# Pairing head h with head h + 4 in the last four attention chunks, with split loads of q and k and x written back to neighbours

## The chip, the cores and the metric

The kernel runs on one core of one Trainium2 chip. The metric is the device time of one execution in microseconds (us). Its engines run side by side and meet at semaphores: PE (TensorE, matmuls), PEld (its weight loads), DVE (VectorE), ACT (ScalarE), POOL (GpSimd) and SP (SyncE, which here only issues DMAs). An engine carries out its own instructions in order.

## The reference

The input is q, k and v for 4 batches of 8 heads, 768 positions and 64 values a head. Heads 0, 2 and 6 are retrieval heads with plain causal attention. The other five are streaming heads: a query sees the last 64 positions and the first 4 (the sinks). The result goes through a two-layer MLP.

```
retr = is_retrieval                    # [1, 0, 1, 0, 0, 0, 1, 0]
keep = causal & (retr | pos_k < 4 | pos_q - pos_k < 64)
a = softmax(where(keep, q @ k.T / 8, -1e9))          # per batch and head
x = (a @ v).transpose(0, 2, 1, 3).reshape(3072, 512)
h = x @ w_in                            # 512 -> 2048
out = maximum(0.01 * h, h) @ w_out      # 2048 -> 512
```

## The kernel before

The 3072 rows are worked in 8 chunks of 384 positions, in the order batch 0, batch 1 (first halves), batch 0, batch 1 (second halves), then the same for batches 2 and 3. So chunks 4 and 5 are first halves and 6 and 7 second halves of batches 2 and 3; a second half has more keys.

One loop iteration n does the MLP of chunk n (in_slots at L548, sixteen units of four 384-column matmuls; out_slots at L573, sixteen units of 512-column matmuls, one chunk behind) and, between these units, the attention of chunk n + 1. merge (L606) lays the two lists out by hand. From iteration 3 on, the last nine MLP units come after the last attention slot. In iteration n also the loads of chunk n + 3 and the transposes of chunk n + 2 are issued.

The path of q and k of a chunk is: load_qk (L107) casts fp32 to bf16 during a DMA from POOL's queue, one transfer of 128 KB for each of three position tiles; turn_dma (L221) lets SP issue a DMA transpose of the whole chunk, which puts two heads on the 128 partitions of each of four pairs; spreads (L228) lets DVE copy each half of the keys into a zero-padded buffer kt, so that one pair's q serves either head. load_v and v_shift bring v, once as it is and once shifted by half a tile. load_qk has one buffer for k and one for q, so a chunk's load waits until the transpose before it has read the buffer.

Attention (L275) makes units for each head: retr, with full score tiles, and stream, six 64-column score matmuls. Each unit's scores go through exp on ACT and a mask on DVE, and the AV matmuls (L295) follow two slots later. The units of a pair gather in one PSUM bank po. The sink scores of all heads come from one unit, sink (L301): four matmuls, one for each pair, with ksink as weights, in which every head has four columns of its own. finish (L383) adds the sink AV of a pair (65 columns for a pair with one streaming head, 130 for one with two), takes the reciprocal of the sums and multiplies (L394) into xs. x_t (L397) transposes xs into xt, from chunk 4 on by a DMA transpose that SP issues, one for each pair as soon as it is finished. sink_keys_by (L254) fills ksink: its zeros are set once at the start, and two small copies for each batch put in the keys.

The pairs before are (0, 1), (2, 3), (4, 5), (6, 7): each has at least one streaming head. The lines that order pairs and sinks:

```
for h in order:                                              # order = range(H)
    if seen == {0, 1} or (2 in seen and h == 1):
        units.append((self.sink, None, None))
...
last = {p: max([sink_at] + [j for j, u in enumerate(units) if u[2] == p]) for p in range(4)}
```

Of the kernel before, what the change touches and what calls it, by code (L numbers as in the profile page):

```python
# [12 lines left out]
BF16 = mybir.dt.bfloat16  # L13
ACTF = mybir.ActivationFunctionType
ALU = mybir.AluOpType
# [6 lines left out]
def kernel(  # L22
# [12 lines left out]
    nc = tc.nc  # L35
# [49 lines left out]
    vs = [bf(f"vs{i}", H, D + 1) for i in range(2)]  # L85
    ksink = [bf(f"ksink{i}", 4 * SK) for i in range(2)]
    ats = [bf(f"ats{i}", 3, 4, 64) for i in range(5)]
    ats4 = [bf(f"ats4{i}", 4, 4, 64) for i in range(2)]
    w_in_bf = bf("w_in_bf", KG, DF)
    w_out_bf = bf("w_out_bf", NG, DM)  # L90

# [3 lines left out]
    k0 = rot.tile([128, 3, H, D], BF16, name="k0", tag="kd", bufs=2)  # L95
    q0 = rot.tile([128, 3, H, D], BF16, name="q0", tag="qd", bufs=3)
    f0 = {nm: rot.tile([128, DM], FP32, name="o", tag="o", bufs=6).rearrange("p (h d) -> p h d", h=H) for nm in ("k", "q")}

    def load_first(nm):
        for eng, h in ((nc.sync, slice(0, 4)), (nc.scalar, slice(4, 8))):  # L100
# [6 lines left out]
    def load_qk(n, nms="kq"):  # L107
        b, c = ORDER[n]
        for nm in nms:
            t = rot.tile([128, 3, H, D], BF16, name=f"{nm}b", tag=f"{nm}b", bufs=1)  # L110
            raw[nm, n] = t
            for g in range(3):
                nc.gpsimd.dma_start(out=t[:, g], in_=nat[nm][b, c, :, :, g])  # L113

    def load_v(n, gs=range(3)):
        b, c = ORDER[n]
# [137 lines left out]
    def sink_keys_by(b):  # L254

        ks, kk = ksink[b % 2], kt[b % 2]

        def odd():
            nc.vector.tensor_copy(ks[64:128, :].rearrange("p (q t) -> p q t", t=SK)[:, :, NS : 2 * NS],
                                  kk[64:128, :, 1, 0:NS])  # L260

        def even():
            nc.vector.tensor_copy(ks[0:64, 256 + 4 * NS : 256 + 5 * NS], kk[0:64, 2, 0, 0:NS])

        return [odd, even]

    def sink_keys(b):
        for f in sink_keys_by(b):
# [6 lines left out]
    class Attention:  # L275
        def __init__(self, n, score_tags=("psS",), po_tags=("po", "po", "po", "po"), xt_eng="a", cross=False):
            self.n = n
            self.b, self.c = ORDER[n]
            self.i = self.b % 2
            xts[n] = rot.tile([128, 4, CH], BF16, name="xt", tag="xt", bufs=2)  # L280
            self.po = {}
            self.tags = score_tags
            self.po_tags = po_tags
            self.sc = 0
            self.xt_eng = xt_eng
            self.cross = cross
            self.sink_lo = 128 if self.c == 0 else 0
            self.units = {h: (self.retr(h) if IS_RETR[h] else self.stream(h)) for h in range(H)}
# [12 lines left out]
        def sink(self):  # L301
            i, c = self.i, self.c
            s = self.score()
            w = CH - self.sink_lo
            for p in range(4):
                nc.tensor.matmul(s[:, 0:w], lhsT=ksink[i][:, 128 * p : 128 * p + 128], rhs=q_of(self.n, p, self.sink_lo, CH),  # L306
                                 start=(p == 0), stop=(p == 3))
            self.at_sink = rot.tile([128, CH], BF16, name="at_sink", tag="at_sink", bufs=2)
            nc.scalar.activation(out=self.at_sink[:, self.sink_lo : CH], in_=s[:, 0:w], func=ACTF.Exp, scale=SM)

        def retr(self, h):
            p, hh = divmod(h, 2)
            i, c, n = self.i, self.c, self.n
            groups = [[(0, 0)], [(1, 128), (2, 256)]] if c == 0 else \
                [[(kj, 0)] for kj in range(4)] + [[(4, 128), (5, 256)]]
            r = []
            for grp in groups:
                box = {}

                def qk(grp=grp, box=box):  # L320
                    s = self.score()
                    a = rot.tile([128, CH], BF16, name="at", tag="at", bufs=6)
                    off = 0
                    for j, (kj, lo) in enumerate(grp):
                        w = CH - lo
                        nc.tensor.matmul(  # L326
                            s[:, off : off + w], lhsT=kt[i][:, p, hh, 128 * kj : 128 * kj + 128],
                            rhs=q_of(n, p, lo, CH), start=(j == 0), stop=(j == len(grp) - 1),
                            skip_group_check=True)
                        off += w  # L330
                    nc.scalar.activation(out=a[:, 0:off], in_=s[:, 0:off], func=ACTF.Exp, scale=SM)  # L331
                    if len(grp) == 2:
                        d = a.rearrange("p (j t) -> p j t", j=3)[:, 0:3:2, :]
                        nc.vector.tensor_mul(d, d, m_caus.rearrange("p (o t) -> p o t", o=1).to_broadcast([128, 2, 128]))  # L334
                    elif grp[0][0] >= 3 * c:
                        nc.vector.tensor_mul(a[:, 0:128], a[:, 0:128], m_caus[:])  # L336
                    box[0] = a

                def do_av(grp=grp, box=box):
                    off = 0  # L340
                    for (kj, lo) in grp:
                        for qi in range(lo // 128, 3):
                            o = off + 128 * qi - lo
                            self.av(p, hh, qi, box[0][:, o : o + 128], va[self.b][:, kj, h, :])
                        off += CH - lo

                r.append((qk, do_av, p))
            return r

        def stream(self, h):  # L350
            p, hh = divmod(h, 2)
            i, c, n = self.i, self.c, self.n
            box = {}

            def qk():
                s = self.score()
                a = ats[ats_i[0] % len(ats)]
                ats_i[0] += 1
                for m in range(6):
                    k0 = 64 * max(6 * c + m - 1, 0)  # L360
                    nc.tensor.matmul(  # L361
                        s[:, 64 * m : 64 * m + 64], lhsT=kt[i][:, p, hh, k0 : k0 + 128],
                        rhs=q_of(n, p, 64 * m, 64 * m + 64), start=(m == 0), stop=(m == 5),
                        skip_group_check=True)
                av_ = a[:, :, 0:4:3, :]
                nc.scalar.activation(  # L366
                    out=av_, in_=s[:, 0:CH].rearrange("p (j e f) -> p j e f", j=3, e=2),
                    func=ACTF.Exp, scale=SM)
                m_ = (m_win0 if c == 0 else m_win).rearrange("p (j e) f -> p j e f", j=3)
                nc.vector.tensor_mul(av_, av_, m_)  # L370
                box[0] = a

            def do_av():
                a = box[0]
                for j in range(3):
                    t = 3 * c + j
                    ve = va[self.b][:, 0, h, :] if t == 0 else vb[self.b][:, t - 1, h, :]
                    self.av(p, hh, j, a[:, j, 0:2, :], ve)
                    self.av(p, hh, j, a[:, j, 2:4, :], va[self.b][:, t, h, :])

            return [(qk, do_av, p)]

        def finish(self, p):  # L383
            for j in range(self.sink_lo // 128, 3):
                a = self.at_sink[:, 128 * j : 128 * j + 128]
                if IS_RETR[2 * p]:
                    self.av(p, 1, j, a, vs[self.i][:, 2 * p + 1, :])
                else:
                    self.av(p, None, j, a, vs[self.i][:, 2 * p : 2 * p + 2, :])
            po = self.po[p]  # L390
            linv = rot.tile([128, 3, 2], FP32, name="linv", tag="linv", bufs=2)
            nc.vector.reciprocal(linv[:], po[:, :, :, D])  # L392
            xs = rot.tile([128, 3, 2, D], BF16, name="xs", tag="xs", bufs=4)
            nc.vector.tensor_tensor(xs[:], po[:, :, :, 0:D], linv.to_broadcast([128, 3, 2, D]), op=ALU.mult)  # L394
            return xs

        def x_t(self, p, xs, tag="psS", eng="a"):  # L397
            if self.cross:
                nc.sync.dma_start_transpose(out=xts[self.n][:, p, :].rearrange("p (j t) -> p j t", j=3),
                                            in_=xs.rearrange("p j h d -> p (j h d)"))  # L400
# [6 lines left out]
            else:  # L407
                nc.vector.tensor_copy(xts[self.n][:, p, :], pt[:, 0, 0:3, :])

        def slots(self, order=range(H), lag=2):  # L410
            units = []
            seen = set()
            for h in order:
                if seen == {0, 1} or (2 in seen and h == 1):
                    units.append((self.sink, None, None))
                seen.add(h)
                units += self.units[h]
            sink_at = [j for j, u in enumerate(units) if u[1] is None][0]
            last = {p: max([sink_at] + [j for j, u in enumerate(units) if u[2] == p]) for p in range(4)}
            LAG, X = lag, 0 if self.cross else 3  # L420
            r, box = [], {}
            for t in range(len(units) + LAG + X):
# [23 lines left out]
    class First:  # L446
        def __init__(self, j):
# [1 line left out]
            self.at_of, self.po, self.xs = {}, {}, {}  # L449
            self.qs = slice(128 * j, 128 * j + 128)  # L450
            if j == 0:
                self.at = rot.tile([128, H, 128], BF16, name="at8", tag="at8", bufs=1)
            else:
                self.blocks = [(kj, h) for kj in range(j, -1, -1) for h in RETR] + [None]
                self.at = bf(f"at_first{j}", len(self.blocks), 128)
# [364 lines left out]
```

## Time and profile before

| | us |
|---|---|
| median of 9 runs | 235.99 |
| lowest, highest | 235.22, 236.66 |
| the profiled execution's own time | 235.35 |
| its span, first to last instruction | 233.6 |
| busy in the span: PE | 224.5 |
| ACT | 127.8 |
| DVE | 97.1 |
| POOL (its DMA issues included) | 71.5 |

The granted TensorE clock was 1.00 of full speed. The busy times are sums over the whole span; what a change is worth in one stage has to be read from the timeline of that stage. A merged line of the timeline gives the start, the length and how many instructions were put together; some matmul records (a few per cent) are missing, so a group of three can show as two. A name like kt<-kd reads "kt written from kd".

### The profile page before, as it was taken

How to read it: one execution, taken by the hardware profiler on the slowest of the kernel's cores; microseconds unless marked ns; L12 is line 12 of the kernel's file. 1: busy time of each engine (PE TensorE's matmuls, PEld its weight loads, DVE VectorE, ACT ScalarE, POOL GpSimd, SP SyncE). 2: the span in 40 equal slices, each digit the busy share in tenths (PEclk: the TensorE clock that was granted, in tenths of full speed). 3: DMA queues.
4: the chain of work that ended last, by engine and by line, in shares of the span. 5: the costliest groups of instructions: out<-in, count | busy, mean ns of one | idle time of the engine just before them, and what ended most of it. 6: DMA issues, size and time to landing. Idle time of an engine off the chain costs nothing.

```text
span 233.6 us, 5091 instructions
## 1 busy us (share of the span) xinstructions
PE 224.5 (96%) x2054; PEld 140.0 (60%) x2080; DVE 97.1 (42%) x281; ACT 127.8 (55%) x276; POOL 71.5 (31%) x87
## 2 busy tenths in 40 slices
PE   8799899999999999999999999999999999999995
PEld 5689566645665676566556655656556665555554
DVE  7778676034456252666324451155213341111122
ACT  4665857714764887655355544766466763434300
POOL 8986625048149069167005800000000000000000
DMA  9999999999999999989949992920210221111112
GB/s 130 151 183 165 203 207 167 175 148 174 143 242 195 167 182 137 184 134 164 129 97 190 175 165 58 207 65 17 79 48 0 65 65 35 45 45 45 45 47 90
DMA packets 109479, 28.97 MB, mean 124 GB/s; under 512 B 101248, under 2 KB 105744, under 8 KB 109456
## 3 DMA queue, kind: packets, MB, share of 16 engines
q0 software_dynamic: 77088, 13.39, 74.6%
q1 hardware_dynamic: 31312, 15.00, 30.7%
q10 hardware_dynamic: 1056, 0.26, 0.6%
q8 instruction: 16, 0.26, 0.5%
q14 instruction: 7, 0.06, 0.1%
HBM read 27.30 MB, written 6.29 MB: 144 GB/s over the span
## 4 chain that ended last, share of the span: by engine, by line
PE 92%; ACT 3%; DVE 2%; issue 1%
PE py L580 31%; PE ph L554 30%; PE po L295 6%; PE psS L326 5%; PE psS L580 3%; PE psS L361 3%; PE ph L567 2%; PE psS L554 2%; PE psS L151 2%; PE psS L306 2%; ACT at L331 1%; PE py L213 1%; PE psS L404 1%; ACT g L556 1%; PE po L511 1%
## 5 line engine op out<-in xcount | busy, mean ns | idle before, releaser
L554 PE MATMUL ph<-xt,w_in_bf 128*128 128x384 bf16 x448 | 90.5, 326 | 0.0
L580 PE MATMUL py<-w_out_bf,g 128*128 128x512 bf16 (+1 forms) x326 | 85.7, 374 | 1.4
L556 ACT ACTIVATE g<-ph 128x384 bf16<-128x384 f32 x112 | 55.0, 492 | 56.6 <-PE ph L554 55.9
L554 PEld LDWEIGHTS <-w_in_bf 128*128 128x128 bf16 x480 | 44.1, 98 | 31.2 <-issue 0.2
L580 PEld LDWEIGHTS <-g 128*128 128x128 bf16 x416 | 35.7, 98 | 25.6
L331 ACT ACTIVATE at<-psS 128x384 bf16<-128x384 f32 x78 | 36.7, 490 | 15.7 <-PE psS L326 15.4
L586 DVE COPY o<-py 128x512 f32<-128x512 f32 (+1 forms) x22 | 14.9, 679 | 53.0 <-PE py L580 52.6
L113 POOL DMA_DIRECT2D kb<-in_k_dram x21 | 18.7, 904 | 39.0 <-DMA kd<-kb 38.0
L326 PE MATMUL psS<-qd,kt 128*128 128x384 bf16 (+2 forms) x90 | 22.8, 294 | 0.0
L118 POOL DMA_DIRECT2D va<-in_v_dram x24 | 21.5, 919 | 2.5 <-DMA w_out_bf<-in_moe_w_out_dram 1.8
L113 POOL DMA_DIRECT2D qb<-in_q_dram x21 | 18.6, 913 | 5.4 <-DMA w_in_bf<-in_moe_w_in_dram 1.8
L295 PE MATMUL po<-va,at 128*128 128x65 bf16 x228 | 19.4, 193 | 0.0
L370 DVE TENSOR_TENSOR ats<-ats,m_win 128x384 bf16<-128x384 bf16 x35 | 12.9, 376 | 15.3 <-ACT ats L366 15.0
L366 ACT ACTIVATE ats<-psS 128x384 bf16<-128x384 f32 x35 | 16.8, 488 | 3.4 <-PE psS L361 3.1
L295 PEld LDWEIGHTS <-at 128*128 128x128 bf16 x234 | 15.1, 98 | 5.6 <-DVE at L334 0.3
L394 DVE TENSOR_TENSOR xs<-po,linv 128x384 bf16<-128x384 f32 x27 | 15.0, 557 | 0.9
L326 PEld LDWEIGHTS <-kt 128*128 128x128 bf16 x99 | 9.4, 97 | 8.5 <-issue 1.2
L361 PEld LDWEIGHTS <-kt 128*128 128x128 bf16 x210 | 10.5, 98 | 5.8 <-issue 1.0
L336 DVE TENSOR_TENSOR at<-at,m_caus 128x128 bf16<-128x128 bf16 x21 | 4.7, 225 | 22.1 <-ACT at L331 22.1
L234 DVE COPY kt<-kd 64x512 bf16<-64x512 bf16 x36 | 12.8, 355 | 0.6
L295 PEld LDWEIGHTS <-ats 128*128 128x128 bf16 x210 | 10.2, 97 | 3.6 <-DVE xs L394 0.5
L392 DVE RECIPROCAL linv<-po 128x6 f32<-128x6 f32 x27 | 5.2, 193 | 15.4 <-PE po L295 15.4
(141 smaller groups left out, 206.1 us busy)
## 6 DMA issues: line engine op xcount, KB each, us to landing
out_dram<-o SPq DMA_DIRECT2D x23, 256.0 KB, 2.5
va<-in_v_dram POOLq DMA_DIRECT2D x24, 128.0 KB, 7.7
kb<-in_k_dram POOLq DMA_DIRECT2D x21, 128.0 KB, 5.8
qb<-in_q_dram POOLq DMA_DIRECT2D x21, 128.0 KB, 6.2
w_in_bf<-in_moe_w_in_dram POOLq DMA_DIRECT2D x4, 512.0 KB, 9.3
w_out_bf<-in_moe_w_out_dram POOLq DMA_DIRECT2D x4, 512.0 KB, 12.7
vb<-va SPq DMA_DIRECT2D x8, 195.0 KB, 4.0
vb<-va SPq DMA_DIRECT2D x4, 130.0 KB, 3.6
```

The lines of the kernel that those rows point to most:

```text
L113: nc.gpsimd.dma_start(out=t[:, g], in_=nat[nm][b, c, :, :, g])
L118: nc.gpsimd.dma_start(out=va[b][:, 3 * c + g, :, 0:D], in_=nat["v"][b, c, :, :, g])
L295: nc.tensor.matmul(o, lhsT=lhsT, rhs=rhs, start=first, stop=False, skip_group_check=True)
L326: nc.tensor.matmul(s[:, off : off + w], lhsT=kt[i][:, p, hh, 128 * kj : 128 * kj + 128], rhs=q_of(n, p, lo, CH), start=(j == 0), stop=(j = ...
L331: nc.scalar.activation(out=a[:, 0:off], in_=s[:, 0:off], func=ACTF.Exp, scale=SM)
L361: nc.tensor.matmul(s[:, 64 * m : 64 * m + 64], lhsT=kt[i][:, p, hh, k0 : k0 + 128], rhs=q_of(n, p, 64 * m, 64 * m + 64), start=(m == 0), s ...
L366: nc.scalar.activation(out=av_, in_=s[:, 0:CH].rearrange("p (j e f) -> p j e f", j=3, e=2), func=ACTF.Exp, scale=SM)
L394: nc.vector.tensor_tensor(xs[:], po[:, :, :, 0:D], linv.to_broadcast([128, 3, 2, D]), op=ALU.mult)
L554: nc.tensor.matmul(ph[:, 0:CH], lhsT=w_in_bf[:, g, 128 * t : 128 * t + 128], rhs=xts[n][:, g, :], start=(g == 0), stop=(g == KG - 1))
L556: nc.scalar.activation(out=gs[n][:, t, :], in_=ph[:, 0:CH], func=ACTF.Prelu, alpha=0.01)
L580: nc.tensor.matmul(py[n][:, 0 : c1 - c0], lhsT=gs[n][:, ng, 128 * tt : 128 * tt + 128], rhs=w_out_bf[:, ng, c0:c1], start=(ng == 0), stop= ...
L586: nc.vector.tensor_copy(o[:, 0 : c1 - c0], py[n][:, 0 : c1 - c0])
```

## The change

For chunks 4 to 7 (`far`) the pairs become (0, 4), (1, 5), (2, 6), (3, 7). Pair (2, 6) has two retrieval heads, so it has no sink score matmul and no sink AV. The order of heads in these chunks is 0, 4, 1, 5, 2, 6, 3, 7, with the sink unit after head 4.

To bring the two heads of a new pair side by side, each load of q and k is issued as two transfers of four heads, into every other place of the tile. ksink is laid out anew for batches 2 and 3: a memset and three small copies instead of two copies. finish writes the two heads of a pair into different parts of a new tile xs8, next to those of the neighbouring pair, and x_t issues two DMA transposes after pair 1 and two after pair 3. The tiles ats4 and at8 (used at the start only) move into the rotating slots of the output tile o, which makes room for xs8.

The core of the diff:

```diff
-    ats4 = [bf(f"ats4{i}", 4, 4, 64) for i in range(2)]
+    ats4 = [rot.tile([128, 4, 4, 64], BF16, name="ats4", tag="o", bufs=6) for i in range(2)]
+    def far(n):
+        return n >= 4
+    def place(n, h):
+        return (h % 4, h // 4) if far(n) else divmod(h, 2)
...
             for g in range(3):
-                nc.gpsimd.dma_start(out=t[:, g], in_=nat[nm][b, c, :, :, g])
+                if far(n):
+                    for a in range(2):
+                        nc.gpsimd.dma_start(out=t[:, g, a : H : 2], in_=nat[nm][b, c, :, 4 * a : 4 * a + 4, g])
+                else:
+                    nc.gpsimd.dma_start(out=t[:, g], in_=nat[nm][b, c, :, :, g])
...
-        return [odd, even]
+        def far_rows():
+            nc.vector.memset(ks[:], 0.0)
+            w = 128 + NS
+            nc.vector.tensor_copy(ks[64:128, 4 * NS : 4 * NS + 4 * w].rearrange("p (q t) -> p q t", t=w)[:, :, 0:NS],
+                                  kk[64:128, :, 1, 0:NS])
+            for p in (1, 3):
+                nc.vector.tensor_copy(ks[0:64, w * p : w * p + NS], kk[0:64, p, 0, 0:NS])
+        return [far_rows] if b >= 2 else [odd, even]
...
+            self.heads = [[h for h in range(H) if place(n, h)[0] == p] for p in range(4)]
+            self.sunk = [p for p in range(4) if not all(IS_RETR[h] for h in self.heads[p])]
...
-            for p in range(4):
+            for p in self.sunk:
                 nc.tensor.matmul(s[:, 0:w], lhsT=ksink[i][:, 128 * p : 128 * p + 128], rhs=q_of(self.n, p, self.sink_lo, CH),
...
-                if IS_RETR[2 * p]:
-                    self.av(p, 1, j, a, vs[self.i][:, 2 * p + 1, :])
+                h0, h1 = self.heads[p]
+                if p not in self.sunk:
+                    continue
+                if IS_RETR[h0]:
+                    self.av(p, 1, j, a, vs[self.i][:, h1, :])
                 else:
-                    self.av(p, None, j, a, vs[self.i][:, 2 * p : 2 * p + 2, :])
+                    self.av(p, None, j, a, vs[self.i][:, h0 : h1 + 1 : h1 - h0, :])
...
+            if far(self.n):
+                if p == 0:
+                    self.xs8 = rot.tile([128, 4, 3, 2, D], BF16, name="xs8", tag="xs8", bufs=2)
+                nc.vector.tensor_tensor(self.xs8.rearrange("p (a g) j e d -> p g e j a d", a=2)[:, p // 2, p % 2], po[:, :, :, 0:D], linv.to_broadcast([128, 3, 2, D]), op=ALU.mult)
+                return None
...
         def x_t(self, p, xs, tag="psS", eng="a"):
+            if far(self.n):
+                for g in {1: (0, 2), 3: (1, 3)}.get(p, ()):
+                    nc.sync.dma_start_transpose(out=xts[self.n][:, g, :].rearrange("p (j t) -> p j t", j=3),
+                                                in_=self.xs8[:, g].rearrange("p j e d -> p (j e d)"))
+                return
...
+            order = order or ((0, 4, 1, 5, 2, 6, 3, 7) if far(self.n) else range(H))
             for h in order:
-                if seen == {0, 1} or (2 in seen and h == 1):
+                if seen == set(self.heads[0]) or (2 in seen and h == 1):
                     units.append((self.sink, None, None))
...
-            last = {p: max([sink_at] + [j for j, u in enumerate(units) if u[2] == p]) for p in range(4)}
+            last = {p: max([sink_at] * (p in self.sunk) + [j for j, u in enumerate(units) if u[2] == p]) for p in range(4)}
...
-                self.at = rot.tile([128, H, 128], BF16, name="at8", tag="at8", bufs=1)
+                self.at = rot.tile([128, H, 128], BF16, name="at8", tag="o", bufs=6)
```

More of the change, by code (lines that the diff above doesn't have):

```diff
@@ L311, in retr @@
         def retr(self, h):
-            p, hh = divmod(h, 2)
+            p, hh = place(self.n, h)
             i, c, n = self.i, self.c, self.n
@@ L350, in stream @@
         def stream(self, h):
-            p, hh = divmod(h, 2)
+            p, hh = place(self.n, h)
             i, c, n = self.i, self.c, self.n
@@ L408, in x_t, with slots @@
                 nc.vector.tensor_copy(xts[self.n][:, p, :], pt[:, 0, 0:3, :])
-        def slots(self, order=range(H), lag=2):
+        def slots(self, order=None, lag=2):
             units = []
             seen = set()
+            order = order or ((0, 4, 1, 5, 2, 6, 3, 7) if far(self.n) else range(H))
             for h in order:
-                if seen == {0, 1} or (2 in seen and h == 1):
+                if seen == set(self.heads[0]) or (2 in seen and h == 1):
                     units.append((self.sink, None, None))
```

## The prediction

> **What bounds the kernel now.** I read the page's busy shares first, then its chain of waits, then the merged timeline of single engines around the four attention chunks that the change touches (4 to 7).
>
> ```profile
> PE 224.5 (96%) x2054; PEld 140.0 (60%) x2080; DVE 97.1 (42%) x281; ACT 127.8 (55%) x276; POOL 71.5 (31%) x87
> ...
> PE 92%; ACT 3%; DVE 2%; issue 1%
> ```
>
> The second line is the chain that ended last: 92% of it is matmul time on PE, so between 94 and 200 us, where chunks 4 to 7 are attended to, a matmul taken away is worth its own length and a matmul that waits costs the wait. A busy PE need not be a full one, so I read start times. These are the timeline's sink lines, one chunk with 256 columns and one with 384:
>
> ```profile
> 97.72 0.60 PE L306 MATMUL psS<-qd,ksink 128*128 128x256 bf16 x4
> 98.16 0.26 PE L295 MATMUL po<-va,at 128*128 128x65 bf16 x3
> ...
> 148.76 0.81 PE L306 MATMUL psS<-qd,ksink 128*128 128x384 bf16 x4
> 149.41 0.26 PE L295 MATMUL po<-va,at 128*128 128x65 bf16 x3
> 149.50 0.81 PE L554 MATMUL ph<-xt,w_in_bf 128*128 128x384 bf16 x4
> ```
>
> Column one is the start. Four sink score matmuls take 98.16 - 97.72 = 0.44 us (0.110 each) or 149.41 - 148.76 = 0.65 us (0.162 each); three AV matmuls of 65 columns take 0.09 us (0.031 each). Such spacing holds almost everywhere. One place matters where PE does wait, the first slots of chunk 4. VectorE there:
>
> ```profile
> 94.50 1.86 DVE L234 COPY kt<-kd 64x512 bf16<-64x512 bf16 x6
> 96.28 0.17 DVE L259 COPY ksink<-kt 64x16 bf16<-64x16 bf16 x1
> 96.46 0.16 DVE L263 COPY ksink<-kt 64x4 bf16<-64x4 bf16 x1
> 96.53 0.21 DVE L336 TENSOR_TENSOR at<-at,m_caus 128x128 bf16<-128x128 bf16 x1
> ```
>
> and PE's weight loads:
>
> ```profile
> 96.09 0.10 PEld L326 LDWEIGHTS <-kt 128*128 128x128 bf16 x1 [0.35 <-DVE kt L234]
> ...
> 96.95 0.16 PEld L295 LDWEIGHTS <-at 128*128 128x128 bf16 x3
> ```
>
> The keys of chunk 4 are spread by six copies only when its scores are due: the load at 96.09 waits for the fifth copy (its end is 0.05 us earlier). The AV weights at 96.95 need the mask at 96.53, which ends at 96.74: slack 0.16 us. So here VectorE's queue is on the path.
>
> [...]six key copies beside GpSimd's DMA issues took 2.45 us, six with none beside them 1.86:
>
> ```profile
> 72.58 2.45 DVE L234 COPY kt<-kd 64x512 bf16<-64x512 bf16 x6
> ```
>
> [...]
>
> **The change, part by part.**
>
> Sinks, on PE. Pair (2, 6) drops out: one score matmul less per chunk, 2 x 0.110 (chunks 4, 5) + 2 x 0.162 (6, 7) = 0.54 us. The sink AVs go per query tile from 65 + 65 + 65 + 130 columns to 65 + 130 + 130, that is from 3 x 0.031 + 0.057 = 0.150 to 0.031 + 2 x 0.057 = 0.145; over 2 + 2 + 3 + 3 tiles 0.05 us. PE work removed: 0.6 us. The other matmuls are the same in number and shape. The new head order keeps three short stream units close together and the sink unit in nearly the same slot; the LAG of two slots is unchanged: 0, from -0.3 (the one late mask of chunk 6, where PE waits 0.3 at 165.3, gone) to +0.3 (another).
>
> Sink keys, on VectorE. Batches 2 and 3 get a memset (row L171: 285 ns) and three small copies (0.17 each at most) in place of two. Starts are about 0.13 to 0.18 apart, so it is 0.4 us more per batch. Batch 3's lie late in chunk 4, where VectorE waits for PE 1.17 us at 113.49: hidden. Batch 2's lie at 96.28, between the last key copy and the first mask: of 0.4 the slack hides 0.16, and 0.25 to 0.3 goes to PE. Behind it on VectorE queue the masks of the first two units, and AV matmuls wait for these.
>
> Loads, on GpSimd's queue. 24 loads of 128 KB become 48 of 64 KB. A 64 KB load isn't in the trace. From above: 0.89 (full row kb). From below: 0.59 (row vsf, 32 runs). The weight loads have the same count of runs (4 x 128) and took 0.75 to 0.85; I take 0.78, so 12 x 0.78 - 6 x 0.89 = 4.0 us more per chunk (from 1.8 to 5.3). Runs keep their 128 bytes, and v's loads, already strided in the destination, cost the same 0.9: no extra DMA time taken. Now the collision. GpSimd before:
>
> ```profile
> 84.67 2.72 POOL L113 DMA_DIRECT2D kb<-in_k_dram  x3 [0.57 <-DMA kd<-kb]
> 87.36 2.65 POOL L113 DMA_DIRECT2D qb<-in_q_dram  x3
> 89.96 2.68 POOL L118 DMA_DIRECT2D va<-in_v_dram  x3
> 92.56 0.67 POOL L124 DMA_DIRECT2D vsf<-in_v_dram  x1
> 96.95 1.08 POOL L128 TENSOR_TENSOR vs<-vsf,m_sink 32x448 bf16<-32x448 f32 x1 [3.73 <-DMA vsf<-in_v_dram]
> ```
>
> It was quiet from 93.2 to 96.95, just when the six key copies ran. With 4.0 us more it issues until about 97.3, later still if load 4 starts load 5 late. The copies then take 2.45 instead of 1.86: 0.59 us more, and PE waits for the fifth of them: +0.6 (from 0, [...]to +1.0, if memset and small copies are held too).
>
> What else waits for the later loads: on SP, the transposes of chunk 5 (95.12 and 96.78) and the v shift behind them (98.81) may slip 0 to 3 us; queued behind on SP are an output store and chunk 4's x transposes, which are due later. GpSimd's next load waits for the k transpose. VectorE's first key copy of chunk 5 (102.17) needs that transpose too, which was in flight 5.6 us from 95.12: 0 taken, up to +1.
>
> x written to neighbours. The multiply writes 128 byte pieces: same elements, 557 ns, 0. Four transposes per chunk remain, but pairs 0 and 1 go together, and two follow the last pair instead of one: SP's queue ends 1.18 us later. The cover is nine units of MLP work:
>
> ```profile
> 114.31 1.18 SPq L399 DMA_TRANSPOSE xt<-xs  x1
> ...
> 120.16 0.81 PE L554 MATMUL ph<-xt,w_in_bf 128*128 128x384 bf16 x4
> ```
>
> The last transpose was issued at 114.31 and landed 3.6 us later (the DMA issues of that window), 117.9; chunk 4's first MLP matmul is at 120.16: slack 2.2 us, of which 1.2 is used. The same pair elsewhere is looser (139.12 to 145.13, 166.89 to 172.90, 194.34 to 200.03). 0 taken.
>
> Storage. ats4 and at8 take three slots of tag o that no output needs before the first store (63.90 us): 0.
>
> Sum: -0.6 + 0.3 + 0.6 = **+0.3 us**. The profiled execution took 235.35 (span 233.6 and 1.75 around it), so its like would be 235.65; the median of the runs, 235.99, stands 0.64 above it, and the forecast for the median is 236.3. A measurement of this kernel can tell about 0.3%, 0.7 us, from no change.
>
> **Rivals.**
>
> A (my forecast, 0.45): gain on PE given back at chunk 4's start, 236.3, spread 235.8 to 237.1.
>
> B (0.27): the start of chunk 4 isn't delayed, [...]the waits of 0.17 and 0.35 us already there absorb it. Then only the 0.6 counts: 235.4, or 235.1 with the late mask of chunk 6 gone too. For it: 3 of 6 copies beside DMA issues kept their 0.29. Against: the slack of 0.16 is smaller than the 0.4 of VectorE work.
>
> C (0.28), slower: the last x transposes land too late. A transpose issued while loads flowed was in flight 6.9 us (issue at 106.95) against 2.3 in a quiet stage (166.89). The second of the last pair is issued at about 115.5; it has 120.16 - 115.5 = 4.7 us. If load 6, now issued until about 114 instead of 109.2, still flows, it needs up to 6.9: PE waits 0 to 2.2 us at chunk 4's MLP, on top of A: 236.3 to 238.5, say 237.5. It decides once time in flight passes 4.7 us. Against: the bytes are the same, and load 6 may have landed by 118.
>
> That the change saves nothing on PE (the sink matmuls hidden) is against the start times above; it would be A plus 0.6, 236.9, and lies within A and C.
>
> **Numbers.** Faster by over 0.3%: half of B, 0.13. Within: rest of B, and most of A (0.35), 0.49. Slower: C and A's upper end, 0.38. The range 235.2 to 237.7 takes in B and the lower half of C.
>
> **What would show it.** Right: L306 with four matmuls fewer in chunks 4 to 7 and about 0.6 us less PE work; GpSimd's issues of load 5 past 96 us, rows of about 0.78 us; six key copies near 94.5 taking 2.3 or more; a wait of PEld on kt or at near 96 to 98 grown by 0.5 to 1.2. Wrong: those waits unchanged (B), or a PE wait before the first L554 of chunk 4 or 5 with the last transpose landing just ahead (C).

## The result: 3 us slower, and the profile after

The median went from 235.73 us (32 runs) to 238.98 (10 runs, 237.73 to 240.43); the ratio is 1.0126, with an interval of 1.0102 to 1.0151. So the change costs 3.0 us where +0.3 us, too little to tell from no change, was forecast, and the time lies above the range. Four executions of the kernels below (two of b_split, one each of a_vs and a_spread), each over 1.5% above the fastest of its kernel and at a mean clock of 0.993, are left out of their medians and ratios.

The page of the kernel after, its busy shares, the chain that ended last and the rows of the split loads (busy us, mean ns of one, idle before):

```profile
PE 224.9 (95%) x2040; PEld 139.7 (59%) x2066; DVE 98.8 (42%) x285; ACT 127.9 (54%) x276; POOL 85.8 (36%) x111
...
PE 79%; DMA 7%; POOL 4%; DVE 4%; ACT 3%; issue 2%; SPq 1%; POOLq 0%
...
L123 POOL DMA_DIRECT2D kb<-in_k_dram x24 | 18.0, 774 | 17.2 <-issue 9.3
...
L123 POOL DMA_DIRECT2D qb<-in_q_dram x24 | 18.0, 798 | 0.0
```

GpSimd is busy for 14.3 us more. Transfers and GpSimd now stand in the chain that was nearly all matmul time before, and VectorE's share in it has grown from 2% to 4%. Of the 7% of transfers, though, 4% are the first load of w_in, far ahead of the change (see below). The three sink matmuls of a chunk, in PE's timeline:

```profile
101.00 0.49 PE L329 MATMUL psS<-qd,ksink 128*128 128x256 bf16 x3
...
126.85 0.49 PE L329 MATMUL psS<-qd,ksink 128*128 128x256 bf16 x3
...
152.96 0.65 PE L329 MATMUL psS<-qd,ksink 128*128 128x384 bf16 x3
```

They are three where there were four, and these starts serve as a ruler. I take the distance from the sink start of one chunk to that of the next, and at the end to the start of the last matmul. From chunk 2 on these starts are 57.59, 77.24, 97.72, 122.53, 148.76, 177.18 and 230.52 before, and 58.91, 78.56, 101.00, 126.85, 152.96, 181.23 and 234.41 after:

| from the sink start of chunk | before, us | after, us | difference |
|---|---|---|---|
| 2 to 3 | 19.65 | 19.65 | 0 |
| 3 to 4 | 20.48 | 22.44 | +1.96 |
| 4 to 5 | 24.81 | 25.85 | +1.04 |
| 5 to 6 | 26.22 | 26.11 | -0.11 |
| 6 to 7 | 28.42 | 28.27 | -0.15 |
| 7 to the last matmul | 53.34 | 53.19 | -0.15 |

All the loss lies in two stretches, and their sum with the gains is +2.6 us. The spans of the two profiled executions differ by more (237.5 against 233.6): 1.1 us of that is a wait for the first w_in load near 21 us, far ahead of the change. It comes and goes between executions: b_split, which changes nothing before chunk 4's load, shows 1.09 us of it too, a_one 0.56 and a_vs none.

**The start of chunk 4.** GpSimd (start, length, instruction; load 5 brings chunk 5, load 6 chunk 6):

```profile
86.53 4.55 POOL L123 DMA_DIRECT2D kb<-in_k_dram  x6
91.02 4.50 POOL L123 DMA_DIRECT2D qb<-in_q_dram  x6
95.41 2.74 POOL L130 DMA_DIRECT2D va<-in_v_dram  x3
98.02 0.71 POOL L136 DMA_DIRECT2D vsf<-in_v_dram  x1
107.53 0.93 POOL L140 TENSOR_TENSOR vs<-vsf,m_sink 32x448 bf16<-32x448 f32 x1 [8.79 <-DMA vsf<-in_v_dram]
108.41 4.54 POOL L123 DMA_DIRECT2D kb<-in_k_dram  x6
```

VectorE in the same place:

```profile
95.82 3.39 DVE L246 COPY kt<-kd 64x512 bf16<-64x512 bf16 x6
99.33 0.28 DVE L279 MEMSET ksink<- 128x272 uint32 x1
99.65 0.17 DVE L281 COPY ksink<-kt 64x16 bf16<-64x16 bf16 x1
99.83 0.23 DVE L284 COPY ksink<-kt 64x4 bf16<-64x4 bf16 x2
99.98 0.21 DVE L359 TENSOR_TENSOR at<-at,m_caus 128x128 bf16<-128x128 bf16 x1
```

And PE's weight loads, with the idle time before each in brackets:

```profile
96.57 0.10 PEld L349 LDWEIGHTS <-kt 128*128 128x128 bf16 x1 [0.59 <-DVE kt L246]
...
98.32 0.10 PEld L349 LDWEIGHTS <-kt 128*128 128x128 bf16 x1 [1.15 <-DVE kt L246]
98.94 0.10 PEld L349 LDWEIGHTS <-kt 128*128 128x128 bf16 x1 [0.53 <-DVE kt L246]
...
100.24 0.14 PEld L318 LDWEIGHTS <-at 128*128 128x128 bf16 x3 [0.37 <-DVE at L359]
```

Load 5 issues until 98.7 instead of 93.2, and the six key copies of chunk 4 begin at 95.82, among its v issues. The trace has them one by one:

| v or vsf issue starts | copy starts | so far into the issue | copy takes, us |
|---|---|---|---|
| v, 95.41 | 95.82 | 0.41 | 0.69 |
| v, 96.29 | 96.55 | 0.26 | 0.85 |
| v, 97.16 | 97.41 | 0.25 | 0.86 |
| vsf, 98.02 | 98.30 | 0.28 | 0.29 |
| | 98.60, 98.92 | | 0.28, 0.29 |

Each of the first three was held until some 0.2 us into the next issue (they end at 96.51, 97.40 and 98.27). So six copies need 3.39 us instead of 1.86, and the weight loads wait 0.59 + 1.15 + 0.53 + 0.37 = 2.64 us in this place, against 0.17 + 0.35 = 0.52 before:

```profile
94.83 0.10 PEld L326 LDWEIGHTS <-kt 128*128 128x128 bf16 x1 [0.17 <-DVE kt L234]
```

**The end of chunk 4's attention.** SP's timeline has the key transpose of chunk 5 and the last two x transposes of chunk 4:

```profile
96.51 2.01 SPq L237 DMA_TRANSPOSE kd<-kb  x1
...
117.61 2.54 SPq L431 DMA_TRANSPOSE xt<-xs  x2
```

The DMA issues of windows that begin at 96.5 and 118.8 (last number: us from issue to landing; for two, the middle of both):

```profile
kd<-kb SPq DMA_TRANSPOSE x1, 9.5
...
xt<-xs SPq DMA_TRANSPOSE x2, 5.7
```

Before, the same key transpose and the load behind it:

```profile
95.12 1.48 SPq L225 DMA_TRANSPOSE kd<-kb  x1
...
kd<-kb SPq DMA_TRANSPOSE x1, 5.6
...
101.25 2.71 POOL L113 DMA_DIRECT2D kb<-in_k_dram  x3 [3.23 <-DMA kd<-kb]
```

And PE at chunk 4's first MLP unit:

```profile
123.32 0.65 PE L591 MATMUL ph<-xt,w_in_bf 128*128 128x384 bf16 x3
124.96 0.32 PE L591 MATMUL ph<-xt,w_in_bf 128*128 128x384 bf16 x1 [0.99 <-DMA xt<-xs]
```

The key transpose was issued while load 5's v transfers were under way, and took 9.5 us (5.6 before); it landed at 106.05 instead of 100.72. Load 6 starts at 108.41 instead of 101.25. Before, what it waited for last was this transpose, which reads its buffer. Here it was the multiply ahead of it in GpSimd's queue: that waits for the v sink rows of load 5 (vsf), which were in flight 9.4 us and landed at 107.39. So load 6's v issues begin at 117.29, ahead of the last two x transposes (issued 117.61 and 118.86). The first of these landed at 122.94, in time; the second was in flight 6.1 us and landed at 124.9, and PE waits for it with the fourth matmul of the first MLP unit. No run takes the pairing of the transposes out of the kernel after, so its share in this wait is not known.

### The profile page after: what moved, and what is told of

Same layout as the page of the kernel before. It is cut to its first block, busy times and chain, and to the rows that moved or that the text cites. A ratio compares the mean times of both kernels' runs of the same rounds, so it can differ in the third digit from the quotient of the medians.

```text
span 237.5 us, 5087 instructions
## 1 busy us (share of the span) xinstructions
PE 224.9 (95%) x2040; PEld 139.7 (59%) x2066; DVE 98.8 (42%) x285; ACT 127.9 (54%) x276; POOL 85.8 (36%) x111
## 4 chain that ended last, share of the span: by engine, by line
PE 79%; DMA 7%; POOL 4%; DVE 4%; ACT 3%; issue 2%; SPq 1%; POOLq 0%
PE py L617 28%; PE ph L591 27%; PE po L318 6%; PE psS L349 5%; DMA w_in_bf<-in_moe_w_in_dram 4%; PE psS L617 3%; PE psS L384 3%; DMA xt<-xs 3%; PE psS L591 2%; PE psS L329 1%; DVE kt L246 1%; PE ph L604 1%; POOL va L130 1%; POOL kb L125 1%; ACT at L354 1%
## 5 line engine op out<-in xcount | busy, mean ns | idle before, releaser
L123 POOL DMA_DIRECT2D kb<-in_k_dram x24 | 18.0, 774 | 17.2 <-issue 9.3
L123 POOL DMA_DIRECT2D qb<-in_q_dram x24 | 18.0, 798 | 0.0
L246 DVE COPY kt<-kd 64x512 bf16<-64x512 bf16 x36 | 14.1, 391 | 1.3 <-DMA kd<-kb 0.7
L125 POOL DMA_DIRECT2D kb<-in_k_dram x9 | 8.0, 909 | 10.0 <-DMA kd<-kb 9.5
L318 PE MATMUL po<-va,ats 128*128 128x65 bf16 x116 | 11.2, 194 | 0.1
```

The lines of the kernel that those rows point to most:

```text
L123: nc.gpsimd.dma_start(out=t[:, g, a : H : 2], in_=nat[nm][b, c, :, 4 * a : 4 * a + 4, g])
L246: nc.vector.tensor_copy(kt[b % 2][r, :, hh, o : o + 128], raw["kx", n][r, g])
L318: nc.tensor.matmul(o, lhsT=lhsT, rhs=rhs, start=first, stop=False, skip_group_check=True)
```

## The experiments

The theory to test: the split of the loads is the cause, by way of GpSimd's longer queue. Its rivals: the sink keys' new layout, the transposes two by two, and, within the theory, which of the two stretches is the root. "Start" and "end" below are the differences to the kernel before in the distances 3 to 4 and 4 to 5 of the table above. Kernels a_ are edits of the kernel after, kernels b_ of the kernel before.

| kernel | median, us | ratio to before | start | end | six key copies, us |
|---|---|---|---|---|---|
| after | 238.98 | 1.0126 [1.0102, 1.0151] | +1.96 | +1.04 | 3.39 |
| a_one | 236.00 | 1.0008 [0.9985, 1.0031] | +0.68 | -0.11 | 1.84 |
| a_one5 | 236.54 | 1.0027 [1.0005, 1.0048] | +1.20 | +0.98 | 2.63 |
| a_vs | 236.70 | 1.0032 [1.0011, 1.0053] | +1.33 | -0.11 | 2.76 |
| a_spread | 235.72 | 0.9987 [0.9964, 1.0009] | -0.19 | -0.11 | early |
| a_vs_spread | 235.71 | 0.9986 [0.9965, 1.0007] | -0.19 | -0.11 | early |
| a_cover | 238.87 | 1.0115 [1.0073, 1.0157] | +3.27 | +0.71 | 3.63 |
| b_split | 237.27 | 1.0057 [1.0036, 1.0079] | +0.48 | 0 | 2.25 |
| b_split67 | 235.84 | 0.9996 [0.9975, 1.0018] | +0.01 | 0 | as before |
| b_xlate | 236.27 | 1.0012 [0.9996, 1.0029] | 0 | 0 | as before |
| b_far | 236.86 | 1.0040 [1.0016, 1.0064] | +1.19 | 0 | 1.84 |
| b_far_vs | 236.53 | 1.0034 [1.0016, 1.0053] | +0.54 | 0 | 1.84 |
| b_spread | 235.69 | 0.9996 [0.9974, 1.0017] | -0.19 | 0 | early |

The kernel before had medians of 235.77 to 235.82 beside them; the ratios are to these (that of after is to 235.73). In a_cover one MLP unit (0.65 us) has moved from the first distance to the second, so its two differences are +3.9 and +0.1 for the same work.

**a_one: the kernel after with whole loads.**

```diff
-                if far(n):
-                    for a in range(2):
-                        nc.gpsimd.dma_start(out=t[:, g, a : H : 2], in_=nat[nm][b, c, :, 4 * a : 4 * a + 4, g])
-                else:
-                    nc.gpsimd.dma_start(out=t[:, g], in_=nat[nm][b, c, :, :, g])
+                nc.gpsimd.dma_start(out=t[:, g], in_=nat[nm][b, c, :, :, g])
```

> The changed kernel with q and k of chunks 4 to 7 loaded in one transfer per tile again, in plain head order (so pairs get other heads than they are masked for; the work is the same in kind and number, the output is not the reference's). Theory 1 (the extra transfers keep GpSimd's queue issuing over the key copies of chunk 4 and push its loads and the k transpose of chunk 5 back): nearly all of the +3.0 us is gone and the removed sink work shows, about 235.4 us, six key copies of chunk 4 in about 1.9 us, no PE wait on the last x transpose. Theory 2 (the paired x transposes and the sink-key work do it): still 237.5 to 239.

The 3.0 us are gone; by the interval at most 0.7 of them are left. VectorE, and the one wait of PE's weight loads that is longer than before:

```profile
94.91 1.84 DVE L242 COPY kt<-kd 64x512 bf16<-64x512 bf16 x6
```

```profile
98.06 0.15 PEld L314 LDWEIGHTS <-at 128*128 128x128 bf16 x3 [0.64 <-DVE at L355]
```

The copies are back at 1.84, and PE no longer waits for x. Everything else of the change together comes out about even: 0.68 us lost to the sink keys at the start, where a small copy of theirs took 0.45 us beside GpSimd's multiply (0.17 alone), and 0.53 won by the sinks that are left out.

**b_split: the kernel before with chunks 4 to 7 loaded in two transfers of four neighbouring heads each.**

```diff
-                nc.gpsimd.dma_start(out=t[:, g], in_=nat[nm][b, c, :, :, g])
+                if n >= 4:
+                    for a in range(2):
+                        nc.gpsimd.dma_start(out=t[:, g, 4 * a : 4 * a + 4], in_=nat[nm][b, c, :, 4 * a : 4 * a + 4, g])
+                else:
+                    nc.gpsimd.dma_start(out=t[:, g], in_=nat[nm][b, c, :, :, g])
```

> The kernel before with the loads of q and k of chunks 4 to 7 cut into two transfers of four adjacent heads, nothing else. Theory 1: slower by 2 to 3.5 us, about 238.2, with the six key copies of chunk 4 over 3 us and a late x transpose or a late k transpose of chunk 5. Theory 2: within 0.7 us of before.

It is slower by 1.3 us by the ratio, between the two expectations and about half of the 2.8 that the split costs in the kernel after (after against a_one). Its pieces land in neighbouring places of the tile, but the issues are as long as there (0.76 to 0.84 us). The profiled run (236.79) shows only 0.5 us at the start; where the rest of the 1.3 lies in the other runs is not known:

```profile
95.46 2.25 DVE L238 COPY kt<-kd 64x512 bf16<-64x512 bf16 x6
```

All six copies lie over q issues here, and yet only every other one was held: those that began 0.14 to 0.22 us after the start of an issue took 0.27 to 0.29, the others, begun later in it, 0.39 to 0.46. The key transpose of chunk 5 lands at 105.25, as late as in the kernel after, but the last x transpose is issued at 115.75 and landed at 120.37, without a wait. So a late key transpose alone doesn't make x late. The same split costs 2.8 us or 1.3 by what else is in its neighbourhood: the parts don't add.

**b_xlate: the kernel before with its x transposes issued two by two.**

```diff
-                                if self.cross:
+                                if self.cross and p % 2:
+                                    self.x_t(p - 1, box[p - 1])
                                     self.x_t(p, box[p])
```

> The kernel before with the x transposes of chunks 4 to 7 issued two by two, after pair 1 and after pair 3, nothing else. Theory 1: hidden by the nine MLP units, 235.7 plus or minus 0.4. Theory 2: PE waits for the second transpose at the first MLP unit of chunk 4, about 1.2 us slower, 236.9.

No wait for x, and the distances of the ruler are the same to 0.01 us: hidden, when nothing else has changed. The median is 0.45 us above that of before, just outside the 0.4 that was expected, but the ratio's interval includes 1, and the profiled run has 0.7 us of the early wait for w_in.

**b_far: the kernel before with a memset and a third small copy.**

```diff
-        return [odd, even]
+        def far_rows():
+            nc.vector.memset(ks[:], 0.0)
+            odd()
+            even()
+            even()
+
+        return [far_rows] if b >= 2 else [odd, even]
```

> The kernel before with the VectorE work of the new sink keys for batches 2 and 3 (a memset and three small copies instead of two), nothing else. Both theories: 0.2 to 0.4 us slower, about 236.0, as a wait of PE at the first AV matmul of chunk 4; nothing if the slack there is larger than the 0.16 us that I read.

The expectation missed: 1.0 us in the median, 1.2 in the profile. VectorE, GpSimd and the weight load there:

```profile
96.69 0.28 DVE L266 MEMSET ksink<- 128x272 uint32 x1
97.01 0.83 DVE L259 COPY ksink<-kt 64x16 bf16<-64x16 bf16 x1
```

```profile
96.88 0.93 POOL L128 TENSOR_TENSOR vs<-vsf,m_sink 32x448 bf16<-32x448 f32 x1 [3.52 <-DMA vsf<-in_v_dram]
```

```profile
98.39 0.15 PEld L301 LDWEIGHTS <-at 128*128 128x128 bf16 x3 [1.15 <-DVE at L342]
```

The memset took the small copy from 0.7 us ahead of GpSimd's multiply (96.28 and 96.95 before) to 0.1 us behind its start, and a copy of 0.17 took 0.83, until the multiply ended. In the kernel after the multiply came only at 107.53, so the same copy took 0.17 there.

**b_far_vs: the same with the multiply issued behind the loads.**

```diff
                 load_sinks(ORDER[n + 2][0], nc.gpsimd)
-                sink_values(ORDER[n + 2][0], nc.gpsimd)
             if n + 3 < NCH:
                 load_qk(n + 3)
                 load_v(n + 3)
+            if ORDER[n + 2][1] == 0:
+                sink_values(ORDER[n + 2][0], nc.gpsimd)
```

> The kernel before with the added sink-key work on VectorE and with GpSimd's multiply of the sink values issued after the loads of the chunk instead of ahead of them. Theory (the added work costs 1.0 us and not 0.3 because it slides under GpSimd's multiply of 0.93 us, which holds VectorE's small copy): the multiply now runs before the key copies, the PE wait at the first AV matmul of chunk 4 falls from 1.2 to about 0.4 us, and the time from 236.9 to about 236.2. Rival (the length of the added work itself is the cost): unchanged, 236.9.

The small copy:

```profile
96.82 0.17 DVE L259 COPY ksink<-kt 64x16 bf16<-64x16 bf16 x1
```

The start loses 0.54 instead of 1.19. The median fell by 0.3 us only, and the two intervals overlap: the profile confirms the hold, the times only in part.

**a_vs: the kernel after with that same move.** The diff is the one of b_far_vs. It lets load 5 start without waiting behind a multiply for the v sink rows.

> The changed kernel with GpSimd's multiply of the sink values issued after the loads of the chunk instead of ahead of them, so that the loads of chunk 5 needn't wait for the sink rows. Theory 1 (GpSimd's queue is too long at chunk 4): loads of chunk 5 end about 3 us earlier (96 instead of 98.7), most key copies of chunk 4 run undisturbed, the k transpose of chunk 5 lands before 103, no wait on the x transpose: 236 to 237. Rival (the DMA engines, not the queue, are full): under 0.7 us gained.

GpSimd's queue, and the copies:

```profile
83.21 4.49 POOL L123 DMA_DIRECT2D kb<-in_k_dram  x6 [3.06 <-DMA kd<-kb]
```

```profile
94.38 2.76 DVE L246 COPY kt<-kd 64x512 bf16<-64x512 bf16 x6
```

Load 5 starts 3.3 us earlier, the copies take 2.76, the key transpose of chunk 5 lands at 102.43, the last x transpose at 120.0 without a wait. The move also takes the multiply out of load 6's way: that starts at 102.97 instead of 108.41, and its v issues, from 111.94, come well ahead of the last x transposes (116.39 and 117.62). With the same instructions in another order in one queue, the time falls by 2.3 us. So it is when GpSimd issues that costs, and not how much is loaded.

**a_spread: the kernel after with chunk 4's key copies and sink keys laid between the last units of iteration 2**, where VectorE waits for PE.

```diff
-        run(merge(ms[: len(ms) - len(rest)], a), rest)
+        every = merge(ms[: len(ms) - len(rest)], a) + rest
+        if n == 2:
+            every = every[: len(every) - len(extra)]
+            for j, f in enumerate(extra):
+                every.insert(len(every) - 10 + j, f)
+        run(every)
```

> The changed kernel with the six key copies and the sink-key work of chunk 4 taken out of its first slots and put between the last units of iteration 2 (their data has landed ten us earlier). Theory S (the wait at the start of chunk 4 is a loss of its own): that wait of about 2 us is gone and the time falls to about 237.0. Theory L (the load queue sets when the x transposes of chunk 4 land): PE comes 2 us earlier to a transpose that lands when it did, the wait at chunk 4's first MLP unit grows by as much, and the time stays near 238.5.

Both expectations missed: the whole loss is gone. VectorE's last early copies, and the first key copy of chunk 5:

```profile
92.43 1.47 DVE L246 COPY kt<-kd 64x512 bf16<-64x512 bf16 x4
...
105.56 0.29 DVE L246 COPY kt<-kd 64x512 bf16<-64x512 bf16 x1 [3.19 <-DMA kd<-kb]
```

The key transpose of chunk 5 still lands at 105.5, VectorE waits 3.19 us for it, and PE doesn't notice. Load 6 is hardly earlier (107.99). But with the start 2.2 us sooner, the x transposes are issued at 114.67 and 115.90, ahead of load 6's v issues (from 116.93), and land at 118.9 and 120.0: the last one is in flight 4.1 us, not 6.1. So the wait at the end hangs on the delay at the start: the delay puts the transposes behind the v loads. It hangs on load 6 as well: a_vs keeps 1.33 us of the delay, but with its early load 6 the last x transpose is in flight for 2.4 us and PE doesn't wait.

**a_one5: the kernel after with only chunk 5 loaded whole.** The edit is `if far(n) and n != 5:` in the loads.

> The changed kernel with the loads of chunk 5 alone in one transfer per tile and plain head order (its pairs get other heads than they are masked for; the same work, the output is not the reference's); chunks 4, 6 and 7 stay split. Theory (the collision at chunk 4's start is that of the loads of chunk 5): most of the loss of the split is gone, 236.0 to 236.7, key copies of chunk 4 under 2.2 us. Rival (all four chunks' longer queues add up): half of it stays, 237.3 or more.

Three quarters of the loss are gone in the median, but the copies took 2.63 where less than 2.2 was expected, and the profiled run (237.49, at the upper end) still has the wait for x:

```profile
123.07 0.32 PE L591 MATMUL ph<-xt,w_in_bf 128*128 128x384 bf16 x1 [0.93 <-DMA xt<-xs]
```

Load 4, still split, makes load 5 late (from 88.33 instead of 84.67). One chunk's split reaches the next through the one queue.

**b_split67: the split in chunks 6 and 7 alone**, with `n >= 6` in the diff of b_split.

> The kernel before with only the loads of chunks 6 and 7 split. Theory: their later landing is hidden, 235.8 plus or minus 0.4. Rival (the queues of all chunks add up): about half of what splitting all four cost the kernel before (+1.6 us), 236.6.

Nothing (+0.01 us at the start, 0 at the end): what those loads take on GpSimd is hidden. The cost is in loads 4 and 5.

**a_cover: twelve MLP units, not nine, behind chunk 4's last attention slot.**

```diff
-        rest = ms[-9:] if a and n > 2 else []
+        rest = ms[-12 if n == 3 else -9:] if a and n > 2 else []
```

> The changed kernel with twelve instead of nine MLP units behind the last attention slot of chunk 4, so that the last x transposes have about 2 us more. If the wait on the x transpose is a loss of its own: 1.0 us less, about 238.0, with no wait at chunk 4's first MLP unit. If the denser attention slots wait more for their masks: no gain.

The wait for x is gone in the profile and the time is not. The first attention slots now come earlier against load 5 (copies from 94.34, four of them held, 3.63 in all), and PE's clock fell. The windows of 3 us, with the length, busy time (and instructions) of PE, PEld, DVE, ACT and POOL, then the granted clock, DMA share and GB/s:

```profile
94.00:97.00 3.00, 1.61 (x8) 0.41 (x5) 2.92 (x5) 0.99 (x3) 3.00 (x4) 1.00 1.26 151
97.00:100.00 3.00, 2.07 (x15) 1.34 (x17) 1.95 (x9) 1.18 (x3) 0.82 (x2) 0.63 1.48 137
100.00:103.00 3.00, 3.00 (x27) 1.82 (x27) 0.36 (x1) 1.30 (x4) 0.00 (x0) 0.81 1.92 158
```

Three of its five runs show a mean clock of 0.993 (238.87, 239.50, 239.52), the two at full clock took 238.08 and 238.51, no better than the kernel after at full clock. Five runs, with two things changed at once, don't say what more cover is worth: inconclusive.

**b_spread and a_vs_spread: the early copies in the kernel before; both repairs in the kernel after.**

> The kernel before with chunk 4's key copies and sink-key copies put between the last units of iteration 2, nothing else. Theory: the two waits of 0.17 and 0.35 us on the key copies go, 0.3 to 0.5 us faster, about 235.4; the moved copies run beside GpSimd's DMA issues there and may hold VectorE's masks: then no gain.

> The changed kernel with both repairs: chunk 4's key copies between the last units of iteration 2, and GpSimd's multiply of the sink values after the loads. The first alone gave about the time of before (235.7) with single runs up to 238.9, because the k transpose of chunk 5 still landed at 105.5 and VectorE waited 3.2 us for it; with the loads 3 us earlier that wait should go: 235.1, 0.3% faster than before, and a narrower spread. If the multiply now falls on the moved copies: 235.7 again.

b_spread gains 0.19 us at the start in the profile, less than was expected, and nothing that the times can show. a_vs_spread's first key copy of chunk 5:

```profile
102.18 0.28 DVE L246 COPY kt<-kd 64x512 bf16<-64x512 bf16 x1 [0.48 <-DMA kd<-kb]
```

By the ruler it is 0.7 us shorter than the kernel before; its fastest run is 234.51 against 235.04. The median is 235.71 against 235.77, where 235.1 was expected, the spread is no narrower, and the ratio's interval includes 1: it beats the kernel after by 1.4%, and whether it beats the kernel before is not settled.

## Why the prediction was wrong

**Right: what the sinks are worth.** 0.11 in chunks 4 and 5 each and 0.15 in 6 and 7 each, 0.53 us where 0.59 was reckoned (before, the two 130-column sink AVs at 108.46 hold PE for 0.12 us, 0.06 each, as the 0.057 of the sum has it). **Right: the price of an issue**, 0.774 and 0.798 us in the rows of kb and qb against 0.78. Hidden as forecast: the transposes two by two (b_xlate), the loads of chunks 6 and 7 (b_split67). The collision stood in the right place, and the waits on kt and at that were to show it did.

**Mis-sized: the key copies.** The term "copies take 2.45 instead of 1.86" came from one row, and its bound of +1.0 was too low: they took 3.39, and the term of +0.6 is +1.5. Six copies took 1.84 us with GpSimd quiet (a_one) and 3.39 here, but an issue did not hold every copy that met it: those that began early in an issue passed. In the row that I used, at 72.58, a held copy was let go 0.10 to 0.16 us into the next issue, so that the copy behind it began at 0.13 to 0.20 and passed: every other one was held. Here the release came at 0.22 to 0.24, the next copy began at 0.25 or 0.26, and was held again, three in a row. The average of one row was no price for this; the bound from above, as an estimate, is one issue for each copy that can meet one (the three held here took 0.69 to 0.86 us, beside v issues 0.87 us apart).

**Nearly right, but by luck: the sink keys.** +0.3 was for VectorE's instructions by their own lengths. In the kernel after it is 1.96 - 1.53 = 0.43. The multiply that could hold them was not thought of: where it does it is 0.68 (a_one) and 1.19 (b_far). In the kernel after the late load 5 had pushed that multiply out of the way.

**The step that failed: "0 taken" for what waits for the later loads**, and with it "load 6 may have landed by 118". The key transpose may slip, it says, and what the slip does to load 6 was not carried into the sum. It did slip, by 1.4 us at its issue, but by 5.3 at its landing, now that it ran among load 5's v transfers: it was in flight 9.5 us instead of 5.6, and the last two of them 9.4 and 9.5 us instead of 4.8 and 4.9. The v sink rows were late with it, the multiply waits for them, and load 6 stands behind the multiply: it came 7 us later, issued until 120.0 and not 114, and its last v transfer landed at 124.9. This is rival C, and its criterion was good: past 4.7 us in flight PE waits; 6.1 us were measured, and PE waited 1.0 us (1.15 by the ruler). It was given a chance of 0.28 and left out of the forecast. But the same long queue feeds A and C: a_spread took away the delay at the start and C went with it. A came without C in a_vs and b_split; C came in no run without A. Either miss alone, +0.9 for the copies or +1.15 for x, would have left 236.3 inside the range.

Against the sum of the prediction: -0.5 for the sinks, +1.96 at the start in place of +0.9, +1.15 at the end in place of 0, together +2.6. The rest of the 3.0 is spread between runs: of the ten, four show a mean clock of 0.991 to 0.993 and a median of 239.5, the other six 238.4, 2.7 us above before, which the sum nearly gives. Why the clock falls in some runs is not settled; nothing of it was in the prediction.

## What to carry to other kernels

Split in two, the loads of k and q of a chunk took their queue 9.0 us to issue instead of 5.3. The lateness went on into the next load in the same queue (load 6 from 108.41 instead of 101.25) and to what was in flight beside the late loads (the key transpose of chunk 5, 9.5 us instead of 5.6). To price work that lies beside GpSimd's issues, lay the new timeline of that queue over VectorE's, and allow for every copy that can meet an issue the length of that issue (an estimate from the copies of 0.69 to 0.86 us above). Before such a change, look for an instruction that waits for data ahead of the loads (here one small multiply) and for copies that could run earlier: moving the multiply gave back 2.3 us of the 3.0 (a_vs), moving the copies all of it (a_spread).

## What the runs showed of the hardware that I had not expected

A copy of 64x512 beside a 64 or 128 KB issue on GpSimd was held or not by when it began. In the traces of all 14 kernels, 110 such copies began within 0.227 us of an issue's start, and all took 0.27 to 0.29 us, as alone; 158 began 0.25 to 0.63 us into an issue, and every one ended 0.08 to 0.13 us after the end of that issue. Of the six in between one passed. The issues of the v sink rows (vsf) held none (12 cases). So 0.22 or 0.25 us into an issue decided between 0.29 and, beside a v issue of the kernel after, 0.85 us.

GpSimd's multiply held even a tiny copy: 64 partitions by 16 elements took 0.83 us (b_far), begun 0.13 us into a multiply of 0.93, and 0.17 alone. A memset begun 0.19 us into one took its usual 0.285 us (a_one).

The same key transpose was in flight 5.6 us when the last v issue lay 3.4 us back (before), 7.4 when it lay 1.3 us back (a_vs), and 9.5 and 9.9 when the v loads were just being issued (after, a_one5). Issued 1.1 us ahead of the first v issue it was in flight for 6.6 (b_split).

PE's clock fell in a_cover: it was 0.50 from 97.75 to 101.15 us, and in the 3.4 us before that PE was busy for 1.30:

```profile
94.35:97.75 3.40, 1.30 (x6) 0.45 (x7) 3.28 (x7) 0.98 (x2) 3.40 (x5) 1.00 1.21 142
97.75:101.15 3.40, 3.18 (x18) 1.84 (x20) 1.60 (x8) 1.36 (x3) 0.07 (x1) 0.50 1.59 155
```

PE never waited for more than 0.9 us at a stretch here. In the kernel after PE was busy for 2.00 of the 3.4 us from 96.85, and the clock stayed at 1.00 in that execution. What makes it fall was not shown. A mean clock of 0.993 over 237 us is what one stretch of 3.4 us at half speed gives (an estimate: 0.5 x 3.4 / 237 = 0.007).
